# Sigmoid attention and a SwiGLU block on one core: transposes queued behind their casts, an earlier weight slice, and three copies shared by two engines

## The chip, the cores and the metric

The kernel runs on one core of a Trainium2 chip. The metric is the device time of one execution in microseconds (us); lower is better. The core has five engines that run side by side and meet only through semaphores: TensorE (PE in the profile, its weight loads PEld), VectorE (DVE), ScalarE (ACT), GpSimd (POOL) and SyncE (SP). SP computes nothing here; it issues transfers, in program order. POOL issues transfers too, also in program order with its own computing.

## The reference

```python
# q, k, v: (8, 12, 448, 64) float32
scores = scale * q @ k.T - log(448)          # scale = 1/8
attn   = 1 / (1 + exp(-scores))              # sigmoid attention, no row sums
x      = (attn @ v) -> (3584, 768)           # 8*448 tokens, 12 heads side by side
g      = x @ w_gate                          # 768 x 1536
out    = (g * sigmoid(g) * (x @ w_val)) @ w_out   # 1536 x 768, result (3584, 768) float32
```

## The kernel before, in words

**Attention is cut into quads.** A quad `n` is four heads of one batch entry: 8 batch entries times `NJ` = 3 quads give `NQ` = 24. For each quad, `fetch(n)` issues three loads on POOL's queue: q and k in float32 into the staging tile `stg_a` (four slots, two quads), and v, converted on the way, into `v` (five buffers). `casts(n)` are two POOL instructions (line 190) that turn q and k into bf16 tiles `c` (pool `c16`, four buffers, so two quads). `trans(n)` issues two DMA transposes on SP's queue (line 197) from `c` into `T` (pool `qkT`, three buffers for q and three for k). `ready(n)` is `casts(n)` followed by `trans(n)`. The first four quads are prepared in other ways during the ramp.

From `T` the PE makes score tiles `(n, c)`, seven per quad (line 239); ACT applies the sigmoid to each (`sig_tile`, lines 255 and 258) into `pt_a`; `pv(n)` multiplies with v on the PE (line 272), 28 matmuls, and copies the result to `xT` tiles: one 128x448 copy (line 281) and two of 64x448 (line 286). A parameter `how` of `pv` gives one of the two small copies to ACT (line 297, `how` = 1) in place of DVE; then `pv` returns a function `rest` that has to be called to make that copy.

**The block runs beside it.** `ffn1(b, f)` makes the gate and value products of batch entry `b` and hidden slice `f` (line 311), ACT the sigmoid (line 329), DVE the products (lines 331 and 335), giving `hT`. The second product of a pair of batch entries `pb` is made by one plain tile or several, `ffn2(pb, m)` (24 matmuls at line 606, then two DVE copies with a scale at line 619, one for each half of 384 columns, into an `osb` tile), and by `ffn2_group(pb, g)`, a Strassen-like form that makes two output tiles from seven half-size products (line 548, DVE at lines 559 and 565). There are six plain tiles: three for `pb` 0 and one for each other `pb`. The last `pb` uses a seven-product form for the first product as well (`double`, line 415). `osb` has four buffers; each is written out by two stores on SP's queue (line 518).

**PSUM** is a ring of four tiles of two banks (`ps_D`), handed out in program order by `Banked`. A unit waits until the earlier user of its tile has been read.

**The order is written out by hand.** Two lists are merged by estimated times: the units (`ffn1`, `ffn2`, ...) and the *visits*, groups of three or four score tiles: visit `(n, 0)` holds tiles 0 to 3 of quad `n`, visit `(n, 4)` tiles 4 to 6. After a visit that holds tile `(n, c)`, what stands in the dictionary `plan` under `(n, c)` is issued. For the later quads, `plan` puts `casts(n + 2)` and `fetch(n + 3)` at `(n, 4)`, and `trans(n + 2)` one visit later, at `(n + 1, 0)`. Stores of the units between those two visits are issued on SP's queue ahead of the transposes. For quads 6 to 9 `plan` calls `ready`, and `hold(n)`, a copy of one column out of `T` on POOL (line 734), makes POOL wait until the transposes of quad `n` have landed before the next `fetch`. `w_out(i)` loads slice `i` of four of the output weights (`wo`, line 130), also on POOL's queue. In `pb` 0's output stage `w_sum` (line 476) makes differences of those slices on DVE.

In the main loop a finished quad's `pv` is postponed to the next visit, or, ahead of certain units, issued alone; the flag `how` is true only for the second unit after the last visit, the last Strassen group of `pb` 2; in front of it the last quad's `pv(23)` is issued. Three operations of `x_sums` on POOL and the units `double` come after it.

Of the kernel before, what the change touches and what calls it, by code (L numbers as in the profile page):

```python
# [13 lines left out]
MULT = mybir.AluOpType.mult  # L14
# [6 lines left out]
def kernel(  # L21
# [10 lines left out]
    nc = tc.nc  # L32
    ctx.enter_context(tc.manual_schedule())

    B, H, S, D = q.shape
# [9 lines left out]
    hsc = lambda pb: 512.0 if pb in FAST else 4096.0  # L45
# [67 lines left out]
    def apart(second, *firsts):  # L113

        for first in firsts:
            keys[0] += 1
            tc.add_to_no_dep_group(f"half{keys[0]}", first.ins)
            tc.declare_no_dep(second.ins, group=f"half{keys[0]}", reason="another bank or other partitions")
# [102 lines left out]
    def trans_pe(n):  # L221
        D2 = Banked()
        ds = [qkT.tile([128, C, 128], BF16, tag=f"T{w}", name=f"T{w}_{n}") for w in range(2)]
        for f in [trans_part(D2, w, n, w, 0, C, nc.vector, ds[w]) for w in range(2)]:
            f()
        qT[(n, 0)] = ds[0]
# [34 lines left out]
    def pv(n, how=0, at=None):  # L261

        b, j = divmod(n, NJ)
        P = Banked(at=at).t
        vt = v16.pop(n)
        for c in range(C):
            pt = pts.pop((n, c))
            for h2 in range(2):
                for w in range(2):
                    r = slice(w * 64, w * 64 + 64)  # L270
                    g = (w ^ h2) * 64
                    nc.tensor.matmul(  # L272
                        out=P[g:g + 64, h2, :S],
                        lhsT=vt[r, h2, c * D:(c + 1) * D],
                        rhs=pt[r, h2, :],
                        start=(c == 0),
                        stop=(c == C - 1),
                    )

        x = xtp.tile([128, S], FP16, tag="xT", name=f"xT_{b}_{2 * j}")  # L280
        first = nc.vector.tensor_copy(out=x, in_=P[:, 0, :S])  # L281
        xT[(b, 2 * j)] = x
        x = xtp.tile([128, S], FP16, tag="xT", name=f"xT_{b}_{2 * j + 1}")
        xT[(b, 2 * j + 1)] = x
        halves = [(x[w * 64:(w + 1) * 64, :], P[(1 - w) * 64:(2 - w) * 64, 1, :S]) for w in range(2)]
        done = [nc.vector.tensor_copy(out=o, in_=i) for o, i in halves[how:]]  # L286
        if how == 2:
            for o, i in halves:
                apart(nc.scalar.copy(out=o, in_=i), first)
        sums = lambda: x_sums(b // 2, j) if b // 2 in FAST and b % 2 else None  # L290
        if how != 1:
            sums()

        def rest():
            if how == 1:
                o, i = halves[0]
                apart(nc.scalar.copy(out=o, in_=i), first, *done)
                sums()

        return rest  # L300


    V, G = nc.vector, nc.gpsimd
# [43 lines left out]
    hw = DM // 2  # L347
# [25 lines left out]
    def early_w(s):  # L373
        for kind in (3, 1, 2, 4):
            for i in range(JT):
                fast_w(s, kind, i)
# [3 lines left out]
    def x_sums(pb, j):  # L380

        a11, a12 = xT[(2 * pb, 2 * j)], xT[(2 * pb, 2 * j + 1)]
        a21, a22 = xT[(2 * pb + 1, 2 * j)], xT[(2 * pb + 1, 2 * j + 1)]
        if j == 0:
            ts = [half_of(ramp_a)[:, 8 * FW * hw + i * S:8 * FW * hw + (i + 1) * S] for i in range(3)]
        else:
            ts = [xtp.tile([128, S], FP16, tag="xT", name=f"xS{i}_{pb}_{j}") for i in range(3)]
        s1, s2, s4 = ts
        eng = G if j else V
        eng.tensor_tensor(out=s1, in0=a21, in1=a22, op=ADD)  # L390
        eng.tensor_tensor(out=s2, in0=s1, in1=a11, op=SUB)
        eng.tensor_tensor(out=a21, in0=a11, in1=a21, op=SUB)  # L392
        eng.tensor_tensor(out=s4, in0=a12, in1=s2, op=SUB)
        xS[(pb, j)] = (s1, s2, a21, s4)
# [114 lines left out]
    def store(engs, pb, m, osb, cols):  # L509

        for w in range(2):
            store_half(engs[w], pb, m, w, osb, cols)
# [85 lines left out]
    def ffn2(pb, m):  # L598
        D = Banked("o")

        head, tail = range(NF - 1), (NF - 1,)
        for half, fs in ((0, head), (1, head), (0, tail), (1, tail)):
            for f in fs:
                h = hT[(pb, f)].rearrange("p b s -> p (b s)")
                D.write(
                    nc.tensor.matmul(  # L606
                        out=D.t[:, half, :hw],
                        lhsT=h[:, m * 128:(m + 1) * 128],
                        rhs=wo16[f // FW][:, f % FW, half * hw:(half + 1) * hw],
                        start=(f == 0),  # L610
                        stop=(f == NF - 1),
                    ),
                    half,
                    uses=(pb, f),
                )
        osb = osp.tile([128, DM], FP32, tag="osb", name="osb")
        for half in range(2):
            D.read(
                nc.vector.tensor_scalar(
                    out=osb[:, half * hw:(half + 1) * hw], in0=D.t[:, half, :hw], scalar1=1.0 / hsc(pb), scalar2=None, op0=MULT  # L620
                ),
                half,
            )
        store((nc.sync, nc.sync), pb, m, osb, slice(0, DM))
# [37 lines left out]
    for grp in visits:  # L662
        n, c = grp[0]
# [7 lines left out]
    def attn_step(group, pvs, how):  # L671
        for part in (group[:2], group[2:]):
            scs = [(n, c, qk_tile(n, c)) for n, c in part]
            rest = [pv(pvs.pop(0), how) for _ in range(len(pvs))]
            for i, (n, c, sc) in enumerate(scs):

                sig_tile(n, c, sc, split=len(group) == 4 and part[0] == group[0] and i == 1)
            for f in rest:
                f()
# [121 lines left out]
    for f, Df in enumerate(early):  # L801
# [7 lines left out]
    plan = {  # L809
        (3, 2): ((casts, 5), (post.append, 4)),  # L810
        (3, 4): ((post.append, 5),),
        (4, 0): ((fetch, 6),),
        (4, 4): ((ready, 6),),
        (5, 4): ((hold, 6), (fetch, 7), (w_out, 0)),
        (6, 0): ((ready, 7),),
        (6, 4): ((hold, 7), (fetch, 8), (w_out, 1)),
        (7, 0): ((ready, 8),),
        (7, 4): ((hold, 8), (fetch, 9), (w_out, 2), (w_out, 3)),
        (8, 0): ((ready, 9), (fetch, 10)),
        (8, 4): ((casts, 10),),  # L820
        (9, 0): ((trans, 10), (fetch, 11)),
    }
    for n in range(9, NQ):
        if n + 2 < NQ:
            plan[(n, 4)] = ((casts, n + 2),)
            plan[(n + 1, 0)] = ((trans, n + 2),)
        if n + 3 < NQ:
            plan[(n, 4)] += ((fetch, n + 3),)

# [25 lines left out]
    for at, (fn, args, how) in enumerate(seq):  # L855
        if fn is None:
            pvs, pend = pend, []
            attn_step(args, pvs, how)
            if at == last_visit:
                nc.scalar.preload_act_table(SILU)  # L860
            for n, c in args:
                for act, of in plan.get((n, c), ()):
                    act(of)
                if c == C - 1:
                    pend.append(n)
            while post:
                trans_pe(post.pop())
            continue
        if pend and (fn is ffn1 and args[1] == 0 and (args[0], NP - 1) not in xT or fn is double or how):
            for n in pend:  # L870
                pv(n)
            pend = []
        fn(*args)
        if fn is ffn2 and args == (B // 2 - 2, C - 1):
            G.tensor_copy(out=held[:, :1], in_=hS[(args[0], 4, HF - 1)][:, :1])
            early_w(0)
        if fn is ffn2_group and args == (B // 2 - 2, 0):
            early_w(1)
# [30 lines left out]
```

## Time and profile before

| what | value |
|---|---|
| median of 9 runs | 410.42 us |
| lowest, highest | 408.88, 419.63 us |
| the profiled execution, its own time | 413.47 us |
| its span (first to last instruction) | 410.4 us, so 3.07 us lie around it |
| PE busy | 397.8 us (97%) |
| DVE, ACT, POOL busy | 263.2 (64%), 216.4 (53%), 126.1 us (31%) |
| mean granted PE clock | 0.995 |

The PE is the engine to follow: where it is busy, nothing else can shorten the kernel but less PE work, and where it is idle, the releaser of the next PE instruction names what was late. Idle time on the other engines costs nothing by itself. The profiled execution is itself 3.05 us slower than the median, so a wait seen in it need not have the same length in every run.

### The profile page before, as it was taken

Reading aid. Unit: us, or ns where it says so; the run is one execution under the profiler, and the core shown is the slowest. Engines: PE = TensorE matmul, PEld = TensorE weight load, DVE = VectorE, ACT = ScalarE, POOL = GpSimd, SP = SyncE. Lnnn points to the kernel's source line nnn. Section 1 sums busy time; section 2 is a strip of 40 time slices with the busy share of each in tenths; the row PEclk is TensorE's granted clock in tenths of the full one; section 3 lists DMA queues with packets and bytes.
Section 4 is the critical chain, followed back from the end, with each engine's and each line's share of the span. In section 5 each row is a group of like instructions: output and inputs, shape, how many; then the busy total and the mean of one; then the engine's idle time right before and its main releaser. Section 6 shows DMA issues by size and latency. Waiting matters only on the chain.

```text
span 410.4 us, 7992 instructions
## 1 busy us (share of the span) xinstructions
PE 397.8 (97%) x3158; PEld 206.6 (50%) x3158; DVE 263.2 (64%) x495; ACT 216.4 (53%) x332; POOL 126.1 (31%) x163
## 2 busy tenths in 40 slices
PE   7799999999999899999999999999999999999995
PEld 3345544545555444454555545445455555555563
DVE  2637646778855555677844565468775568996753
ACT  5866786646335474565543556555644325656100
POOL 4528042372621346330012314300019960000000
PEclk9899999999999999999999999999999999999999
DMA  8999969979899999742147799601001530000135
GB/s 260 250 250 249 238 129 136 202 171 228 229 188 160 235 226 169 211 69 91 22 85 205 158 229 158 157 17 30 1 2 46 140 86 0 2 1 0 40 82 148
DMA packets 59844, 54.38 MB, mean 132 GB/s; under 512 B 35744, under 2 KB 53280, under 8 KB 59808
## 3 DMA queue, kind: packets, MB, share of 16 engines
q0 software_dynamic: 18880, 30.94, 35.3%
q1 hardware_dynamic: 40496, 22.62, 27.6%
q8 instruction: 24, 0.39, 0.4%
q10 hardware_dynamic: 432, 0.33, 0.3%
q14 instruction: 12, 0.10, 0.1%
HBM read 47.19 MB, written 11.01 MB: 142 GB/s over the span
## 4 chain that ended last, share of the span: by engine, by line
PE 87%; DMA 8%; DVE 2%; SPq 1%; issue 0%; POOL 0%; DVEq 0%
PE ps_D L311 40%; PE ps_D L548 15%; PE ps_D L415 12%; PE ps_D L272 8%; PE ps_D L239 8%; DMA T<-c 5%; PE ps_D L606 5%; DMA v<-in_v_dram 2%; DMA st<-in_q_dram 1%; SPq L197 1%; DVE xT L286 1%; PE ps_D L209 0%; DVE xT L281 0%; DVE T L215 0%; SPq L518 0%
## 5 line engine op out<-in xcount | busy, mean ns | idle before, releaser
L258 ACT ACTIVATE pt_a<-ps_D 128x896 f16<-128x896 f32 x148 | 127.3, 919 | 77.4 <-PE ps_D L239 75.0
L311 PE MATMUL ps_D<-xT,wg 128*128 128x448 f16 x432 | 95.3, 353 | 0.1
L311 PE MATMUL ps_D<-xT,wv 128*128 128x448 f16 x432 | 94.8, 352 | 0.0
L331 DVE TENSOR_TENSOR t<-ps_D,s 128x448 f16<-128x448 f32 x72 | 44.8, 623 | 54.7 <-ACT s L329 53.5
L190 POOL CAST c<-stg_a 128x896 bf16<-128x896 f32 x40 | 38.3, 966 | 109.3 <-DMA T<-c 62.2
L329 ACT ACTIVATE s<-ps_D 128x448 f16<-128x448 f32 x72 | 39.5, 549 | 52.5 <-PE ps_D L311 45.9
L311 PEld LDWEIGHTS <-wg 128*128 128x128 f16 x432 | 39.6, 98 | 44.6 <-issue 11.3
L311 PEld LDWEIGHTS <-wv 128*128 128x128 f16 x432 | 42.2, 98 | 39.5 <-issue 0.4
L335 DVE SCALAR_TENSOR_TENSOR hT<-ps_D,t 128x448 f16<-128x448 f32 x72 | 45.0, 625 | 7.5
L239 PE MATMUL ps_D<-T,T 64*64 64x448 bf16 x644 | 44.5, 359 | 3.9 <-DMA T<-c 2.0
L272 PE MATMUL ps_D<-pt_a,v 64*64 64x448 f16 x672 | 36.9, 357 | 0.8 <-DMA v<-in_v_dram 0.8
L559 DVE TENSOR_SCALAR osb<-ps_D 128x384 f32<-128x384 f32 x43 | 24.0, 557 | 17.7 <-PE ps_D L548 17.0
L548 PEld LDWEIGHTS <-S 128*128 128x128 f16 x264 | 25.8, 98 | 17.8 <-issue 0.8
L548 PE MATMUL ps_D<-ramp_a,S 128*128 128x384 f16 x198 | 34.0, 326 | 0.6 <-DVE osb L559 0.6
L281 DVE CAST xT<-ps_D 128x448 f16<-128x448 f32 x24 | 15.0, 624 | 25.4 <-PE ps_D L272 25.2
L425 ACT ACTIVATE snap<-ps_D 128x448 f32<-128x448 f32 x36 | 18.6, 542 | 19.5 <-POOL xT L392 13.2
L239 PEld LDWEIGHTS <-T 64*64 64x64 bf16 x644 | 15.0, 106 | 26.4 <-issue 16.8
L565 DVE SCALAR_TENSOR_TENSOR osb<-ps_D,osb 128x384 f32<-128x384 f32 x33 | 18.4, 557 | 13.2 <-PE ps_D L548 13.1
L272 PEld LDWEIGHTS <-v 64*64 64x64 f16 x672 | 19.7, 108 | 14.0 <-DMA v<-in_v_dram 1.3
L548 PEld LDWEIGHTS <-hT 128*128 128x128 f16 x198 | 18.7, 98 | 14.6 <-issue 2.9
L286 DVE CAST xT<-ps_D 64x448 f16<-64x448 f32 x41 | 25.5, 621 | 0.7
L183 POOL DMA_DIRECT2D v<-in_v_dram x24 | 17.9, 746 | 25.5 <-PE ps_D L239 24.1
(84 smaller groups left out, 402.9 us busy)
## 6 DMA issues: line engine op xcount, KB each, us to landing
out_dram<-osb SPq DMA_DIRECT2D x52, 192.0 KB, 3.1
stg_a<-in_q_dram POOLq DMA_DIRECT2D x20, 448.0 KB, 4.8
stg_a<-in_k_dram POOLq DMA_DIRECT2D x20, 448.0 KB, 6.3
v<-in_v_dram POOLq DMA_DIRECT2D x24, 224.0 KB, 8.2
wg<-in_moe_w_gate_dram POOLq DMA_DIRECT2D x4, 576.0 KB, 11.9
wv<-in_moe_w_val_dram POOLq DMA_DIRECT2D x4, 576.0 KB, 13.0
wo<-in_moe_w_out_dram POOLq DMA_DIRECT2D x4, 576.0 KB, 8.6
ramp_a<-in_q_dram SPq DMA_DIRECT2D x2, 448.0 KB, 6.4
```

The source lines that it names most:

```text
L190: eng.tensor_copy(out=t.rearrange("p c h d -> p h c d"), in_=st.rearrange("p h (c d) -> p h c d", c=C))
L239: nc.tensor.matmul(out=sc[w * 64:(w + 1) * 64, h2, :S], lhsT=kt[r, w * 64:(w + 1) * 64], rhs=qt[r, :, w * 64:(w + 1) * 64], start=True, st ...
L258: nc.scalar.activation(out=pt, in_=sc[:, :, :S], func=SIGM, bias=sbias, scale=qkscale)
L272: nc.tensor.matmul(out=P[g:g + 64, h2, :S], lhsT=vt[r, h2, c * D:(c + 1) * D], rhs=pt[r, h2, :], start=(c == 0), stop=(c == C - 1),)
L286: done = [nc.vector.tensor_copy(out=o, in_=i) for o, i in halves[how:]]
L311: nc.tensor.matmul(out=D.t[:, i, :S], lhsT=(wg16, wv16)[i][f // FW][:, pr, cs], rhs=xT[(b, pr)], start=(pr == 0), stop=(pr == NP - 1),),
L329: D.read(nc.scalar.activation(out=s16, in_=D.t[:, 0, :S], func=SIGM), 0)
L331: D.read(nc.vector.tensor_tensor(out=t1, in0=D.t[:, 0, :S], in1=s16, op=MULT), 0)
L335: nc.vector.scalar_tensor_tensor(out=hT[(b // 2, f)][:, b % 2, :], in0=D.t[:, 1, :S], scalar=hsc(b // 2), in1=t1, op0=MULT, op1=MULT),
L415: nc.tensor.matmul(out=D.t[:, bank, :S], lhsT=W(f, j), rhs=X(j), start=(start and j == 0), stop=(stop and j == JT - 1), skip_group_check=True,
L548: nc.tensor.matmul(out=D.t[:, bank, :hw], lhsT=l, rhs=B_(i), start=(first and i == 0), stop=(i == HF - 1), skip_group_check=True,),
L559: nc.vector.tensor_scalar(out=o, in0=D.t[:, bank, :hw], scalar1=1.0 / hsc(pb), scalar2=None, op0=MULT), bank
```

## The change

Four edits. The transposes of quads 10 to 23 are issued in the same visit as their casts, at `(n, 4)` in place of `(n + 1, 0)`. The order of casts and loads on POOL does not change by it. The third slice of the output weights is loaded at `(6, 4)`, behind the second slice, in place of `(7, 4)`. In `ffn2` the first half of a plain output tile is copied and scaled by ACT in place of DVE. Where `pv` is issued alone for the last quad (flag `how`), it is called with `how` = 1 and its `rest` at once, so that one 64x448 copy goes to ACT.

```diff
@@ ffn2
         for half in range(2):
+            o, i, by = osb[:, half * hw:(half + 1) * hw], D.t[:, half, :hw], 1.0 / hsc(pb)
             D.read(
-                nc.vector.tensor_scalar(
-                    out=osb[:, half * hw:(half + 1) * hw], in0=D.t[:, half, :hw], scalar1=1.0 / hsc(pb), scalar2=None, op0=MULT
-                ),
+                V.tensor_scalar(out=o, in0=i, scalar1=by, scalar2=None, op0=MULT) if half else
+                nc.scalar.mul(out=o, in_=i, mul=by),
                 half,
             )
@@ plan
-        (6, 4): ((hold, 7), (fetch, 8), (w_out, 1)),
+        (6, 4): ((hold, 7), (fetch, 8), (w_out, 1), (w_out, 2)),
         (7, 0): ((ready, 8),),
-        (7, 4): ((hold, 8), (fetch, 9), (w_out, 2), (w_out, 3)),
+        (7, 4): ((hold, 8), (fetch, 9), (w_out, 3)),
         (8, 0): ((ready, 9), (fetch, 10)),
-        (8, 4): ((casts, 10),),
-        (9, 0): ((trans, 10), (fetch, 11)),
+        (8, 4): ((ready, 10), (fetch, 11)),
     }
     for n in range(9, NQ):
         if n + 2 < NQ:
-            plan[(n, 4)] = ((casts, n + 2),)
-            plan[(n + 1, 0)] = ((trans, n + 2),)
+            plan[(n, 4)] = ((ready, n + 2),)
         if n + 3 < NQ:
             plan[(n, 4)] += ((fetch, n + 3),)
@@ main loop
             for n in pend:
-                pv(n)
+                pv(n, 1 if how else 0)()
             pend = []
```

## The prediction

> **What bounds the kernel now.** I first read the page for the engine and the chain.
>
> ```profile
> PE 397.8 (97%) x3158; PEld 206.6 (50%) x3158; DVE 263.2 (64%) x495; ACT 216.4 (53%) x332; POOL 126.1 (31%) x163
> PE 87%; DMA 8%; DVE 2%; SPq 1%; issue 0%; POOL 0%; DVEq 0%
> L239 PE MATMUL ps_D<-T,T 64*64 64x448 bf16 x644 | 44.5, 359 | 3.9 <-DMA T<-c 2.0 <-DVE T L215 1.2 <-ACT pt_a L258 0.3
> L548 PE MATMUL ps_D<-ramp_a,S 128*128 128x384 f16 x198 | 34.0, 326 | 0.6 <-DVE osb L559 0.6
> ```
>
> The PE is idle for 410.4 - 397.8 = 12.6 us. A table of busy time by stretches of 10 us tells where: 5.5 us before 30, 4.4 after the last matmul, and between 30 and 400 only three stretches are under 10.00: 9.86 (120 to 130), 8.01 (130 to 140) and 9.40 (320 to 330). So the middle holds 0.14 + 1.99 + 0.60 = 2.73 us, and nothing else in the middle can be won without less PE work. The change removes no matmul, and it touches neither end. The timeline names the two large gaps, in brackets:
>
> ```profile
> 137.79 0.57 PE L239 MATMUL ps_D<-T,T 64*64 64x448 bf16 x8 [1.99 <-DMA T<-c]
> ```
> ```profile
> 326.23 0.62 DVE L281 CAST xT<-ps_D 128x448 f16<-128x448 f32 x1 [0.97 <-PE ps_D L272]
> 326.87 1.25 DVE L286 CAST xT<-ps_D 64x448 f16<-64x448 f32 x2
> 328.15 0.56 DVE L559 TENSOR_SCALAR osb<-ps_D 128x384 f32<-128x384 f32 x1
> 328.77 3.08 PE L548 MATMUL ps_D<-ramp_a,S 128*128 128x384 f16 x18 [0.60 <-DVE osb L559]
> ```
>
> The first is visit (11, 0), which waits for a transpose of quad 11. Why that is late stands in SP's timeline and, for the start of each piece, in the chain in order of time:
>
> ```profile
> 104.29 5.57 SPq L518 DMA_DIRECT2D out_dram<-osb  x4
> 109.97 4.84 SPq L197 DMA_TRANSPOSE T<-c  x2
> 114.90 8.24 SPq L518 DMA_DIRECT2D out_dram<-osb  x6
> 123.25 5.45 SPq L197 DMA_TRANSPOSE T<-c  x2
> 130.10 2.44 SPq L518 DMA_DIRECT2D out_dram<-osb  x4
> ```
> ```profile
> 123.25 1.59 SPq L197
> ...
> 124.93 12.82 DMA T<-c
> ```
>
> Quad 11's casts ran on POOL from 105.66 to 108.58, but its transposes stood on SP behind stores that wait for DVE's `osb`, and went out at 123.25 and 124.93. The second landed 12.82 us later, at 137.75; the PE was ready at 135.80. Quad 10 is the same case by a hair: cast by 101.6, issued from 109.97, landed at 121.20, wanted at 121.1 (the 0.14 us). The second gap is DVE's own order after `pv(23)`: three `xT` copies (0.62 us each) stand ahead of the copy at line 559 that must free a PSUM bank.
>
> **What the Trainium skill says.** "Perfetto Trace Analysis", section Optimization Strategy: find the gaps on the contended engine, find which semaphore each waits for, and make that dependency start sooner. That is the reading above. "DMA: Bandwidth & Descriptors", section Queues, rings and completion order: a DMA engine takes its queues in turn, packet by packet. The trace agrees: while loads were queued (93 to 98 us), quad 9's transposes moved about 110 packets per us beside about 112 of the loads; alone (68 to 69) they moved 748. So an early transpose may still land late behind loads, and I price that. "ScalarE: Activation LUTs", section Table sets: plain copies are in every table set, so the copies given to ACT need no further table load. The trace agrees: ACT's snap copies at line 425 run between SILUs, with two loads in all (1.283 us each).
>
> **Part by part.**
>
> *Transposes at (n, 4).* The order of instructions on SP changes from stores x4, T10, x6, T11, x4, T12 to T10, x6, T11, x8, T12 (Tn: the two transposes of quad n). T10 can go at about 101.6, when its casts end; SP is idle then (quad 9's last issue ended at 96.8). T11 stands behind six stores, the last of which waits for the third plain tile (copied by 114.45), so it goes near 115 in place of 123.25: 8 us sooner. With the slowest landing in the trace (13.9 us, quad 9's) the second lands by 115 + 1.6 + 13.9 = 130.5, before 135.8. Both waits go: **-2.13 us** (1.99 + 0.14). T12 keeps its place behind the eight stores, so it is next in line: issued at 132.64 and 136.3, landed 9.2 and 8.8 us later, at 145.1; wanted at 150.05, and with the gap gone at 148.06. Slack 2.9 us. From quad 13 on, the PE waited for none; all go out no later than before. SP also waits for PE now (T of quad n+2 needs quad n-1's buffer): that reader is a visit older than any store queued behind, so no store is held by it. What can hold a store is a late cast: T17's was done by 169.6, T18's by 183.7, long before the stores at 208 and 216. Faster casts afterwards (POOL waited 62.2 us for `T<-c`) only bring loads forward; POOL is on no path there.
>
> *Third weight slice at (6, 4).* One POOL issue (0.80 us) moves ahead of quad 8's casts, where POOL idles 1.48 us for q (75.36): nothing on POOL. Its transfer moves from behind fetch 9 to behind slice two. Slice two took from about 77 to 80.7 at some 175 KB/us, so 576 KB are 3.3 us more load traffic, until 84. T8, which lands at 83.4 before, then gets half the packets for 3.3 us and lands near 86.5. `hold(8)` holds POOL for the same 3 us, so fetch 9, its casts and T9 (issued 88.8 and 90.3) start 3 us later; but the loads ahead of T9 are the slice fewer. T9 landed at 104.2, wanted at 107.2: I take 0, with bounds 0 to +2.3 (a start 5.3 later and again 13.9 to land: 109.5). The slices: two lands sooner; slice four moves up by one transfer and back by the 3 us, so it stays near 97.9; its first matmul is at 100.8.
>
> *Plain tiles.* Six DVE copies (0.55 us) become six on ACT (nearest row: line 425, 542 ns). The PE waited for none of them, so 0 is won directly; the tile is out some 0.5 us sooner. New wait: ACT stands at the tile's end with the next visit's sigmoids behind it, and the PE behind those for a PSUM tile. At `pb` 1:
>
> ```profile
> 207.12 1.02 DVE L619 TENSOR_SCALAR osb<-ps_D 128x384 f32<-128x384 f32 x2 [2.03 <-PE ps_D L606]
> 207.61 0.92 ACT L258 ACTIVATE pt_a<-ps_D 128x896 f16<-128x896 f32 x1 [2.16 <-PE ps_D L239]
> ```
>
> ACT's copy would run 207.1 to 207.66, so the sigmoid starts 0.05 late and ends at 208.6; the PE wants that tile at about 209.15, after `pv`. Covered by 0.5 us at all four places followed by a visit: 0. Without that cover it would be 4 x 0.55 = 2.2.
>
> *PV copy.* DVE does two of the three `xT` copies, so line 559 runs from 327.5 to 328.07; the PE, which ended six more matmuls at 328.17, no longer waits: **-0.60 us** (bounds 0 and -0.60). ACT is idle there (1.23 us of work between 320 and 330). `x_sums` starts on POOL at 331.27 after its own queue either way; the sum that product 6 needs ends at 333.42, wanted at about 335.3 in place of 335.9: covered.
>
> Sum: -2.73 us; 413.47 becomes 410.7 in the profiled execution, 3.05 above the median. The PV wait is fixed durations and counts fully in the median. The transpose wait is a race: the landing had 10.9 us from issue, and the six landings of quads 9 to 11 took 13.2, 13.9, 10.6, 9.7, about 12.5 and 12.8, mean 12.1, so a typical wait is 1.2 to 2.1. I take 1.6: 410.42 - 1.6 - 0.6 = **408.2 us**.
>
> **Rivals.**
>
> *A. The forecast*: both waits go. 407.2 to 409.2. Chance 0.52.
>
> *B. The transpose wait is not there in the median run, or T11 is not really sooner* (POOL or a buffer holds it). For it: the profiled run is 3.05 us slow, and something must be shorter in the others. Against: 4 of 6 landings exceed 10.9. Only 0.6 stays: 409.8. Chance 0.22.
>
> *C. T9 is late at (9, 0)*, behind the moved slice. Decides from a delay of 3.0 us; up to +2.3: 408.2 + 2.3 = 410.5, less where it is partly so. Chance 0.10.
>
> *D. Slower: T12 is late at (12, 0)*, because loads run ahead now and share the DMA engines with it. Decides when T12 lands over 2.9 us later than before. With quad 9's worst issue (6.52 us) and landing (13.9): 132.64 + 6.52 + 13.9 = 153.1, a wait of 5.0: 408.2 + 5.0 = 413.2. For it: quad 9 shows such values. Against: casts 14 wait for T12 itself, so only one fetch can be ahead. Chance 0.11. Unlisted harm: 0.05, near 412.
>
> **How the numbers follow.** 0.3% (1.23 us) is about what a measurement of this kernel can tell from no change: below 409.2 is faster, above 411.6 slower. Faster: A and a third of C, 0.55. Same: B and half of C, 0.27. Slower: D, the rest of C and the unlisted, 0.18. Range: 406.9 (A with a wait of 2.9 us, which is the landing of 13.9 against 10.9, in the median) to 411.9, which leaves out most of D.
>
> **What would show it.** In the profile after: no stretch under 10.00 between 120 and 140; T10 issued near 102 and T11 near 115; no wait of PE at 328, with a line-297 copy on ACT beside DVE's; six scaled copies on ACT of about 0.54 us, and the sigmoid behind each at most 0.1 late. Wrong: a PE wait for `T<-c` at visit (9, 0) or (12, 0), for `pt_a` after a plain tile, or a span that shrinks by 2.7 us while the median doesn't move (then B).

## The result and the profile after

The changed kernel takes 415.05 us in the median (17 runs, 411.06 to 418.67), the kernel before 410.28 us (52 runs, 408.62 to 419.84): 4.8 us or 1.2% slower. The ratio is 1.0099, 95% interval 1.0076 to 1.0121. (Ratios leave out runs more than 1.5% above the fastest of the same kernel, and as a late transfer alone can push a run over that line here, the medians of all runs are given beside them.) The forecast was 408.2 us: a gain of 2.2 us where a loss of 4.8 came.

The page of the kernel after, engines and chain:

```profile
PE 398.5 (97%) x3158; PEld 206.8 (50%) x3158; DVE 259.9 (63%) x488; ACT 219.8 (53%) x339; POOL 125.7 (31%) x163
PE 72%; DMA 21%; POOL 4%; issue 1%; SPq 0%; DVE 0%; POOLq 0%; DVEq 0%
L239 PE MATMUL ps_D<-T,T 64*64 64x448 bf16 x644 | 44.4, 359 | 5.9 <-DMA T<-c 4.2
L548 PE MATMUL ps_D<-ramp_a,S 128*128 128x384 f16 x198 | 34.0, 326 | 0.0
```

The share of transfers in the chain rose from 8% to 21%. The idle time in front of line 548 is 0.0 (it was 0.6), so that part worked; in front of line 239 it grew from 3.9 to 5.9 us. The timeline of the PE shows a single wait between 30 and 404 us:

```profile
97.91 7.97 PE L606 MATMUL ps_D<-wo,hT 128*128 128x384 f16 x48
110.12 0.64 PE L239 MATMUL ps_D<-T,T 64*64 64x448 bf16 x8 [4.24 <-DMA T<-c]
110.53 2.84 PE L272 MATMUL ps_D<-pt_a,v 64*64 64x448 f16 x28
...
114.01 4.07 PE L606 MATMUL ps_D<-wo,hT 128*128 128x384 f16 x24
```

This is visit (9, 0): the PE is ready at 110.12 - 4.24 = 105.88 and waits until a transpose of quad 9 has landed. The gap at (11, 0) is gone. The same place in the kernel before:

```profile
107.20 0.57 PE L239 MATMUL ps_D<-T,T 64*64 64x448 bf16 x8
107.60 1.49 PE L272 MATMUL ps_D<-pt_a,v 64*64 64x448 f16 x28
...
109.41 4.08 PE L606 MATMUL ps_D<-wo,hT 128*128 128x384 f16 x24
```

There is a second loss behind the wait. The 28 matmuls of `pv` take 2.84 us, 1.49 in the kernel before. Busy time by stretch (its length, then PE, PEld, DVE, ACT and POOL, then the granted clock, the DMA share and GB/s; the DMA share can pass 1, as it adds up the times of packets that overlap) names the reason:

```profile
110.50:113.90 3.40, 3.40 (x41) 1.55 (x32) 0.45 (x1) 2.28 (x4) 1.64 (x3) 0.50 0.74 172
```

Half the clock for 3.4 us. From the start of (9, 0) to the next plain tile the PE took 2.21 us before (107.20 to 109.41) and takes 3.89 now (110.12 to 114.01): 1.68 us more. The whole loss at this place is 4.24 + 1.68 = 5.9 us.

The chain in order of time, from 76 us, tells how quad 9 came to be late:

```profile
78.03 9.19 DMA T<-c
...
87.34 0.19 POOL held L734
...
88.57 5.74 DMA stg_a<-in_k_dram
...
94.36 0.94 POOL c L190
...
95.32 14.75 DMA T<-c
```

For the kernel before, line 197 shows the transposes of quad 8 and of quad 9 (how many, min/median/max ns to issue them, start of the first and the last; then the us from issue to landing):

```profile
L197 SPq DMA_TRANSPOSE T<-c x2: 1431/1514/1597, 76.3 to 77.9; - x2
DMA to landing us min/median/max: 5.5/5.8/6.2
...
L197 SPq DMA_TRANSPOSE T<-c x2: 1369/3943/6517, 88.8 to 90.3; - x2
DMA to landing us min/median/max: 13.2/13.6/13.9
```

Quad 8's second transpose now takes 9.19 us to land (5.5 before), with the third weight slice beside it. `hold(8)` on POOL waits for it until 87.3, so fetch 9 starts at 87.82 (83.95 before). The second transpose of quad 9 goes out at 95.32 (90.3 before), and then takes 14.75 us. It took 13.9 before: the start is what moved.

The span grew by only 1.7 us (410.4 to 412.1): the removed waits give 2.7, the new one takes 5.9, and the profiled execution after had a faster ramp, which reached (9, 0) 1.3 us sooner. Between medians the difference is 4.8, which the experiments split into 6.1 lost and 1.3 won.

### The profile page after: what moved, and what is told of

It is laid out like the page before. It is cut to its first block, busy times and chain, and to the rows that moved or that the text cites. A ratio compares the mean times of both kernels' runs of the same rounds, so it can differ in the third digit from the quotient of the medians.

```text
span 412.1 us, 8001 instructions
## 1 busy us (share of the span) xinstructions
PE 398.5 (97%) x3158; PEld 206.8 (50%) x3158; DVE 259.9 (63%) x488; ACT 219.8 (53%) x339; POOL 125.7 (31%) x163
## 4 chain that ended last, share of the span: by engine, by line
PE 72%; DMA 21%; POOL 4%; issue 1%; SPq 0%; DVE 0%; POOLq 0%; DVEq 0%
PE ps_D L311 27%; PE ps_D L548 18%; PE ps_D L415 12%; DMA stg_a<-in_k_dram 11%; DMA T<-c 8%; PE ps_D L239 6%; PE ps_D L272 5%; PE ps_D L606 4%; POOL c L190 2%; DMA ramp_a<-in_q_dram 1%; POOL stg_a L178 1%; POOL wg L133 1%; POOL wv L133 1%; POOL v L183 0%; SPq L161 0%
## 5 line engine op out<-in xcount | busy, mean ns | idle before, releaser
L311 PE MATMUL ps_D<-xT,wg 128*128 128x448 f16 x432 | 95.3, 353 | 0.1
L559 DVE TENSOR_SCALAR osb<-ps_D 128x384 f32<-128x384 f32 x43 | 24.0, 558 | 17.5 <-PE ps_D L548 16.8
L272 PEld LDWEIGHTS <-v 64*64 64x64 f16 x672 | 19.8, 109 | 13.9 <-issue 1.6
## 6 DMA issues: line engine op xcount, KB each, us to landing
wg<-in_moe_w_gate_dram POOLq DMA_DIRECT2D x4, 576.0 KB, 11.9
```

What stands on the lines that cost most here:

```text
L272: nc.tensor.matmul(out=P[g:g + 64, h2, :S], lhsT=vt[r, h2, c * D:(c + 1) * D], rhs=pt[r, h2, :], start=(c == 0), stop=(c == C - 1),)
L311: nc.tensor.matmul(out=D.t[:, i, :S], lhsT=(wg16, wv16)[i][f // FW][:, pr, cs], rhs=xT[(b, pr)], start=(pr == 0), stop=(pr == NP - 1),),
L559: nc.vector.tensor_scalar(out=o, in0=D.t[:, bank, :hw], scalar1=1.0 / hsc(pb), scalar2=None, op0=MULT), bank
```

## The experiments

Each run was measured beside new runs of the kernel before, whose medians lie between 410.1 and 410.8 us; a ratio compares with these.

The first question was which of the edits costs the time. Theory: the moved slice. Rival: the transposes issued sooner.

**The changed kernel without the slice move** (`no_slice`).

```diff
-        (6, 4): ((hold, 7), (fetch, 8), (w_out, 1), (w_out, 2)),
+        (6, 4): ((hold, 7), (fetch, 8), (w_out, 1)),
-        (7, 4): ((hold, 8), (fetch, 9), (w_out, 3)),
+        (7, 4): ((hold, 8), (fetch, 9), (w_out, 2), (w_out, 3)),
```

> The changed kernel with the third weight slice put back to (7, 4). Slice theory (the moved slice delays T8, hold(8), fetch 9 and so the transposes of quad 9, and the PE then idles 4.2 us at visit (9, 0) and runs 1.7 us more at half clock): those 6 us go; the profile has no PE wait for T at (9, 0), none at (11, 0) and none at 328; time 0.6 to 2.7 us under the kernel before, ratio 0.993 to 0.998. Transpose theory (transposes 10 and 11 issued earlier share the DMA engines with the loads and make those of quad 9 late): still 3 us or more slower than before, ratio over 1.007, with the wait at (9, 0).

Measured: 408.94 us (22 runs, 407.94 to 413.51), ratio 0.9966 (0.9940 to 0.9992). Between 30 and 404 us its PE has no wait at all; its page:

```profile
PE   7799999999999999999999999999999999999995
PE 94%; DMA 2%; DVE 1%; ACT 1%; SPq 0%; issue 0%; DVEq 0%; ACTq 0%
```

The other three edits make the kernel faster by 1.3 us in the median; the slice move takes 6.1 (415.05 - 408.94). With the earlier transposes kept, the wait is gone: the rival falls.

**The slice move alone** (`slice_only`): the same two lines changed the other way, in the kernel before.

> The kernel before with the third weight slice alone moved to (6, 4). Slice theory: T8 lands 3 to 4 us later, the second transpose of quad 9 is issued near 95 in place of 90.3 and lands near 110; PE wait of 3 to 4.5 us at (9, 0) and half clock behind it; the wait at (11, 0) may stay; 4 to 6 us slower, ratio 1.010 to 1.015. Transpose theory: within 1 us of the kernel before, ratio 0.998 to 1.002.

Measured: median 415.95 us (22 runs, 409.22 to 425.72), 5.7 over the kernel before. The ratio, in which only its seven fastest runs count, is 1.0052 (1.0012 to 1.0093). Its timeline:

```profile
112.59 0.96 PE L239 MATMUL ps_D<-T,T 64*64 64x448 bf16 x8 [5.65 <-DMA T<-c]
143.64 0.57 PE L239 MATMUL ps_D<-T,T 64*64 64x448 bf16 x8 [1.34 <-DMA T<-c]
```

The wait at (9, 0) is there without the moved transposes, and the two old waits are there too: 1.34 at (11, 0), and 0.60 for line 559 at 334.6. The second transpose of quad 9 was issued at 94.26 and took 18.28 us.

**The moved transposes alone** (`trans_only`), the hunks at (8, 4) and in the loop over `n`.

```diff
-        (8, 4): ((casts, 10),),
-        (9, 0): ((trans, 10), (fetch, 11)),
+        (8, 4): ((ready, 10), (fetch, 11)),
...
-            plan[(n, 4)] = ((casts, n + 2),)
-            plan[(n + 1, 0)] = ((trans, n + 2),)
+            plan[(n, 4)] = ((ready, n + 2),)
```

> The kernel before with the transposes of quads 10 to 23 alone moved behind their casts. Slice theory: transposes 10 near 102 and 11 near 115, the waits of 0.14 and 1.99 us are gone, ratio 0.994 to 1.000. Transpose theory: slower by 3 us or more, ratio over 1.007, with a PE wait for T near 107 or at a later visit.

Measured: median 409.48 us, ratio 0.9980 (0.9954 to 1.0006), not told from 1 by itself. There is no PE wait for `T<-c` in its trace, but this trace alone says little on that: it is of one of its longer executions (413.55 us), in which the PE was late already, by a wait before (9, 0):

```profile
102.72 8.18 PE L606 MATMUL ps_D<-wo,hT 128*128 128x384 f16 x39 [2.72 <-DMA wo<-in_moe_w_out_dram]
```

There a weight slice came late at the first plain tile. So an earlier slice answers to something that does happen, in some executions.

**The copies alone** (`copies_only`), the hunks in `ffn2` and in front of `pv`.

```diff
-                nc.vector.tensor_scalar(
-                    out=osb[:, half * hw:(half + 1) * hw], in0=D.t[:, half, :hw], scalar1=1.0 / hsc(pb), scalar2=None, op0=MULT
-                ),
+                V.tensor_scalar(out=o, in0=i, scalar1=by, scalar2=None, op0=MULT) if half else
+                nc.scalar.mul(out=o, in_=i, mul=by),
...
-                pv(n)
+                pv(n, 1 if how else 0)()
```

> The kernel before with the plain-tile copies and the PV copy alone split over ACT and DVE. Both theories: the 0.60 us PE wait near 328 goes, nothing else moves; 0.6 us faster, ratio 0.9985, which may not be told from 1.

Measured: median 409.16 us, ratio 0.9986 (0.9966 to 1.0005): the 0.6 us expected by the ratio (1.1 by the medians), and within the noise. The wait at 328 is gone. Its trace has a wait that the kernel before's trace didn't have, at (12, 0):

```profile
148.22 0.57 PE L239 MATMUL ps_D<-T,T 64*64 64x448 bf16 x8 [1.33 <-DMA T<-c]
```

The transposes alone and the copies alone add to 0.8 + 0.6 = 1.4 us by their ratios; both together (`no_slice`) gave a ratio of 0.9966, 1.4 us. That fits parts that add up, but with intervals of about 1 us to each side it doesn't show it.

**Each copy by itself** (`pv_only`, `plain_only`), one profiled execution each.

> The kernel before with the PV copy alone shared: the PE wait of 0.60 us near 328 goes.

> The kernel before with the plain-tile copies alone shared: the PE wait of 0.60 us near 328 stays; no new PE wait for a sigmoid (pt_a) behind the plain tiles.

Measured: with the PV copy shared, there is no wait near 328, and one of 0.39 us at 113.6, in front of line 548, for a plain tile's copy at line 619. With the plain tiles shared, the 0.60 stays, and no wait for `pt_a` appears:

```profile
124.58 0.96 PE L239 MATMUL ps_D<-T,T 64*64 64x448 bf16 x8 [4.00 <-DMA T<-c]
332.62 3.08 PE L548 MATMUL ps_D<-ramp_a,S 128*128 128x384 f16 x18 [0.60 <-DVE osb L559]
```

So the 0.60 is the PV copy's. This execution took 416.04 us: with the order of transposes as before, quad 10's second one went out at 110.4, took 14.1 us, and the PE waited 4.00 at (10, 0). The kernel before has the same order, so some of its runs of 414 to 417 us may come about in this way; none of these was profiled.

The second question was how one slice of 576 KB, moved by one quad, makes quad 9 late. Two links were in doubt: `hold(8)`, and fetch 10 beside the transposes.

**Fetch 10 held until quad 9's transposes have landed** (`after_hold9`), in the changed kernel.

```diff
-        (8, 0): ((ready, 9), (fetch, 10)),
+        (8, 0): ((ready, 9), (hold, 9), (fetch, 10)),
```

> The changed kernel with hold(9) put between the transposes of quad 9 and fetch 10, so that POOL issues fetch 10 only when those transposes have landed. If the transposes of quad 9 are late because fetch 10 shares the DMA engines with them: issued near 92.5 and 95.3 as in the changed kernel, they land near 102 in place of 110, and the PE wait of 4.2 us at (9, 0) and the half clock behind it go; fetch 10 starts near 102.5 and quad 10 is still in time; about 409 us, ratio 0.996 to 1.000. If their late issue alone decides (some 14 us to land whatever is beside them): they land near 109 again, and it stays 4 us or more slower than before.

Measured: 410.16 us (14 runs), ratio 1.0002 (0.9979 to 1.0026), 4.9 us under the changed kernel. The transposes of quad 9 went out at 92.1 and 93.9, later by 3.3 and 3.6 us than in the kernel before (92.6 and 95.3 in the changed kernel), and landed in 6.5 and 5.5 us. The view of line 197 for quads 8 and 9:

```profile
L197 SPq DMA_TRANSPOSE T<-c x2: 1291/2436/3582, 75.8 to 77.2; - x2
DMA to landing us min/median/max: 8.4/8.8/9.2
...
L197 SPq DMA_TRANSPOSE T<-c x2: 1523/1600/1677, 92.1 to 93.9; - x2
DMA to landing us min/median/max: 5.5/6.0/6.5
```

Quad 8's (first pair) are still slow behind the slice; quad 9's are not. With nothing of fetch 10 beside them they land at 99.4, seven us before the PE wants them (106.38). From 93.9, a landing of 14.75 us would have been 2.3 us too late. So fetch 10 beside the transposes is part of the cause.

**Without `hold(8)`** (`after_nohold8`), in the changed kernel.

```diff
-        (7, 4): ((hold, 8), (fetch, 9), (w_out, 3)),
+        (7, 4): ((fetch, 9), (w_out, 3)),
```

> The changed kernel without hold(8): fetch 9 is issued right behind quad 8's casts, near 78 in place of 87.8. If the way from the moved slice to quad 9 leads through hold(8): casts 9 near 90, transposes of quad 9 issued near 91 and landed by 105, no PE wait at (9, 0) beyond 1 us; 409 to 411 us. Quad 8's own transposes share the engines with slice and fetch 9 and may land near 90 where the PE wants them at 90.5 to 91.8. If hold(8) is not the link: the wait of 4 us at (9, 0) stays, 414 us or more.

Measured: 415.28 us (6 runs), ratio 1.0114 (1.0076 to 1.0152). The wait moved by one quad:

```profile
96.06 0.96 PE L239 MATMUL ps_D<-T,T 64*64 64x448 bf16 x8 [4.81 <-DMA T<-c]
```

This is (8, 0). Now fetch 9 runs beside quad 8's transposes, and they take 13.6 and 16.8 us. Quad 9's went out at 89.4 and 91.5, the second 3.8 us sooner than in the changed kernel, and landed by 105.5. That fits the link through `hold(8)`. That the PE no longer waited for them says little, as it came to (9, 0) only at 114.27. What the run shows besides is that the hold does a service: without it the same collision happens one quad sooner.

**Both slices at (6, 4)** (`after_two_slices`), in the changed kernel: twice the suspected cause.

```diff
-        (6, 4): ((hold, 7), (fetch, 8), (w_out, 1), (w_out, 2)),
+        (6, 4): ((hold, 7), (fetch, 8), (w_out, 1), (w_out, 2), (w_out, 3)),
-        (7, 4): ((hold, 8), (fetch, 9), (w_out, 3)),
+        (7, 4): ((hold, 8), (fetch, 9)),
```

> The changed kernel with the fourth weight slice moved to (6, 4) too, behind the third: twice the suspected cause. Through hold(8): T8 lands another 3 us later (near 90), fetch 9 is issued near 91, T9 near 97 and 99, landing at 111 to 113; PE wait at (9, 0) of 5 to 7 us; 1 to 4 us slower than the changed kernel, ratio to before 1.013 to 1.022. If the bytes in front of T9 decide and not the hold (the fourth slice no longer stands between fetch 9 and T9): no slower than the changed kernel.

Measured: 409.09 us (20 runs, 408.02 to 410.97), ratio 0.9957 (0.9937 to 0.9976). No PE wait between 30 and 404 us. I had expected 1 to 4 us more than the changed kernel; it is 6 less. The delay of the start came as expected: `hold(8)` held until 90.4, and quad 9's transposes went out at 95.9 and 97.2, later than in the changed kernel:

```profile
L197 SPq DMA_TRANSPOSE T<-c x2: 1221/1233/1245, 95.9 to 97.2; - x2
DMA to landing us min/median/max: 3.3/5.6/7.9
```

But they landed in 3.3 and 7.9 us, the last at 105.1, and the PE wanted it at 106.48. Fetch 10 was issued beside them here too (97.11). So the delay by itself is not what costs: late transposes with a short landing are in time. The fourth slice, left between fetch 9 and quad 9's transposes, belongs to the cause as well.

**Both slices in the kernel before** (`two_slices_only`).

```diff
-        (6, 4): ((hold, 7), (fetch, 8), (w_out, 1)),
+        (6, 4): ((hold, 7), (fetch, 8), (w_out, 1), (w_out, 2), (w_out, 3)),
-        (7, 4): ((hold, 8), (fetch, 9), (w_out, 2), (w_out, 3)),
+        (7, 4): ((hold, 8), (fetch, 9)),
```

> The kernel before with both the third and the fourth slice moved to (6, 4). If the slice that stays between fetch 9 and quad 9's transposes is what makes the single move costly: no wait at (9, 0); the waits at (11, 0) and at 328 stay; within 0.3% of the kernel before, ratio 0.997 to 1.001, beside about 1.014 in the medians for the third slice alone. If two slices are only in time because the transposes of the later quads moved: a wait at (9, 0), ratio over 1.007.

Measured: 410.02 us, ratio 0.9998 (0.9979 to 1.0018). No wait at (9, 0). One slice alone costs 5.7 us in the medians, two cost nothing, whatever the order of the later transposes. Its profiled execution took 416.97 us, with 3.58 us of waiting at (11, 0): the old wait, longer than in the first trace.

**The fourth slice between quad 9's casts and fetch 10** (`after_fourth_later`, and the same kernel again as `fourth_later_2` and `fourth_later_3`).

```diff
-        (7, 4): ((hold, 8), (fetch, 9), (w_out, 3)),
+        (7, 4): ((hold, 8), (fetch, 9)),
-        (8, 0): ((ready, 9), (fetch, 10)),
+        (8, 0): ((ready, 9), (w_out, 3), (fetch, 10)),
```

> The changed kernel with the fourth slice moved from in front of quad 9's casts to between these casts and fetch 10: the same transfers in front of fetch 10, but quad 9's q and k no longer share with the slice, and its transposes then run beside the slice and ahead of most of fetch 10. If the q and k loads beside the transposes make them slow: the second transpose of quad 9 lands within 10 us (by about 104), no wait for T at (9, 0); a wait of 0 to 3 us for the fourth slice at the first plain tile is possible, as that now lands near 100 or later; 408.5 to 412 us. If the bytes queued decide, whatever they are: T9 lands near 109 again, 414 us or more.

Measured: median 413.05 us in two groups (6 runs up to 410.2, 16 from 411.2), ratio 1.0042 (1.0016 to 1.0068). The trace was of an execution of 409.12 us, so two more were profiled:

> The same kernel as after_fourth_later, a second look. If its time is over 411 us: either a PE wait for the fourth slice (wo) near 100, 2 us or more with half clock behind it, and T9 landed in time; or a wait for T at (9, 0), near 107, of 2 us or more, with T9 landed near 109.

> A third look at the same kernel, with the same alternatives.

They took 415.15 and 411.10 us. Each has one wait of the PE, and it is for the slice:

```profile
103.90 8.97 PE L606 MATMUL ps_D<-wo,hT 128*128 128x384 f16 x39 [3.79 <-DMA wo<-in_moe_w_out_dram]
```
```profile
102.44 6.50 PE L606 MATMUL ps_D<-wo,hT 128*128 128x384 f16 x39 [2.76 <-DMA wo<-in_moe_w_out_dram]
```

The second transpose of quad 9 took 12.1, 11.9 and 12.4 us in the three traces and landed between 105.8 and 108.1. That is neither "within 10" nor "109 again": beside a slice and then fetch 10 it is faster than in the changed kernel and slower than with less company. No sharp difference between q, k loads and weights was shown.

**Hold(9) without the slice move** (`no_slice_hold9`), the line of `after_hold9` added to `no_slice`.

> The changed kernel with the slice put back to (7, 4) and hold(9) ahead of fetch 10: a version that may beat both. Transposes of quad 9 land near 99 in place of 104, quad 10's still before 119; no PE wait between 30 and 400 us: median 408 to 409.5, as without hold(9) or a little under, with fewer runs over 411. If fetch 10 comes too late for quad 10: a wait at (10, 0), 410 or more.

Measured: 409.68 us, ratio 0.9986 (0.9963 to 1.0010), 0.7 us over `no_slice` in the median and with 4 of 22 runs over 411.5. The profiled execution (412.57 us) waited 0.62 us for a weight slice and 1.55 us for `osb` at 120.7. Where quad 9 is in time already, holding fetch 10 gained nothing. The second transpose of quad 9 landed in 9.7 us here (13.4 in `no_slice`).

**The best of these**: `no_slice` (408.94 us, ratio 0.9966) and `after_two_slices` (409.09 us, 0.9957) both beat both kernels. They were measured beside different runs of the kernel before (medians 410.27 and 410.76), and their intervals overlap, so they are not told apart. The second has no run over 410.97.

## Why the prediction was wrong, point by point

**The waits that were to go did go.** At (11, 0) and at 328 the PE waits no longer. The PV term, -0.60, is exact in the trace and fits the copies' ratio of 0.9986. The transpose term, taken at -1.6 for a typical run, measures -0.8 (`trans_only`, interval -1.9 to +0.2): twice too large by the middle value, as rival B had it in part, but within the interval. Together they measure 1.4 where 2.2 was forecast.

**The step that failed is the third weight slice**: "I take 0, with bounds 0 to +2.3". It measures about +6 (6.1 from `no_slice`, 5.7 from `slice_only`, in medians; 5.9 in the trace). Its mechanism, rival C (quad 9 late at (9, 0) behind the moved slice), was the right one and was given 0.10 and at most +2.3. Three of its terms were wrong.

- *The cancelling.* I let T9's later start be paid back by "the loads ahead of T9 are the slice fewer". The start moved by more than the 3 us that I took: 3.8 for the first transpose and 5.0 for the second (the bound had 5.3). And the landing of the second didn't shorten; it went from 13.9 to 14.75. The table has that landing in every trace that bears on it, by the weight slices issued between fetch 9 and T9, and by where fetch 10 was issued.

| slices ahead of T9 | fetch 10 issued beside T9 | fetch 10 held until T9 has landed |
|---|---|---|
| two | 13.0 to 14.4 us (six traces, the kernel before and `no_slice` among them) | 9.7 us (`no_slice_hold9`) |
| one | 14.75 us (changed kernel), 18.28 us (`slice_only`), 14.0 us (`after_nohold8`) | 5.5 us (`after_hold9`) |
| none | 7.9 us (`after_two_slices`), 7.8 us (`two_slices_only`) | not tried |

With fetch 10 held, a slice fewer does shorten the landing, as I had it. With fetch 10 beside T9, one slice fewer doesn't, and two slices fewer do. That fetch 10 is issued in the same us as T9 (95.24 and 95.32) was in the order of POOL's instructions, and it was so in the kernel before (89.94 and 90.3), but I priced it only for rival D. The two columns differ by one held load, but each cell of the second rests on one trace.

The other two terms:

- *The moment wanted.* Landing was bounded at 109.5 and measured at 110.07, near enough. But I set it against 107.2, the PE's arrival in one execution; in this one the PE came at 105.88. The slack of 3.0 us (104.2 to 107.2) loses 1.3 by the ramp alone.
- *The clock.* I counted a wait as its own length. A wait of 4.24 us brought 1.68 us more at half clock.

**Rival D** (T12 late at (12, 0)) didn't happen in the changed kernel; a wait of 1.33 there turned up in `copies_only`. **The plain tiles** cost nothing, as forecast: ACT's copies take 0.49 us (forecast 0.54), and at `pb` 1 the sigmoid starts right behind the copy with no wait for `pt_a` on the PE:

```profile
209.46 0.49 ACT L621 ACTIVATE osb<-ps_D 128x384 f32<-128x384 f32 x1 [1.67 <-PE ps_D L606]
209.95 0.92 ACT L258 ACTIVATE pt_a<-ps_D 128x896 f16<-128x896 f32 x1
```

But "the tile is out some 0.5 us sooner" didn't come true. DVE's copy of the second half waits for ACT's copy of the first, here at the third plain tile:

```profile
117.96 0.49 ACT L621 ACTIVATE osb<-ps_D 128x384 f32<-128x384 f32 x1 [2.27 <-PE ps_D L606]
118.48 0.56 DVE L620 TENSOR_SCALAR osb<-ps_D 128x384 f32<-128x384 f32 x1 [1.36 <-ACT osb L621]
```

The profile gives ACT's copy as the releaser at five of the six tiles. The two engines take turns, so a pair lasts some 1.1 us, as with two copies on DVE (1.02 at 207.12). In front of line 559 the two engines do overlap (ACT's 64x448 copy at 328.48, DVE's copies at 328.59 and 329.23), and there the wait went.

**The issue times** were off: T10 went at 105.2 and 110.0 in place of 102, T11 at 120.3 in place of 115. Fetch 10 was issued 5.3 us later than before, and POOL then waited until 109.07 for its k; T11 stands behind stores of the third plain tile, which the PE reached late. In `no_slice` T10 went at 101.5 and 102.8 and T11 at 114.5, as forecast.

**What stays open.** That the slice move costs the 6 us is shown, and that both the slice left ahead of T9 and fetch 10 beside it take part. Why the landing stays at 13 us and more with fetch 10 beside and one slice or two ahead, is some 12 with the fourth slice behind the casts, and 8 with none ahead, is not settled. It isn't a matter of bytes alone: over 98 to 110 us the changed kernel's transfers moved 143 GB/s at a DMA share of 1.14, and before, in the like stretch from 92 to 104, 211 GB/s at 1.04. In `slice_only` they moved 49 GB/s from 98 to 100 and 74 from 100 to 102, at shares of 1.38 and 1.41. Why the mixture is so slow was not tried.

## What to carry to other kernels

Before moving a load, list everything that waits for the queue it joins, including a pacing wait that was put there by design, and follow the delay to the next collision; compare not the bytes but which transfers will now be in flight together. A transfer that gets fewer bytes ahead of it need not land sooner: a later start was not paid back here. A slack read from one execution has to be lessened by the spread of the ramp and of the landing times, both over 1 us here. And price a long PE wait with the slow clock behind it: here it came with each of the six waits of 3.58 us and more.

## What the runs showed of the hardware that I had not expected

- *Landing times of the same transpose spread more than fivefold.* A transpose of a 128x896 tile of quad 9 landed in 3.3 us in `after_two_slices`, with no weight slice ahead of it, and in 18.28 us in `slice_only`, with one ahead and fetch 10 beside it.
- *A long PE wait costs more than itself.* With waits of 3.58 us and more the granted clock was 0.50, for 3.4 us (4.24 and 5.65 us of wait) or about 6.8 (3.58, 3.79, 4.00 and 4.81). With 2.72 us it fell in one trace and with 2.76 it stayed at 1.00 in another; after 30 us, no wait of 1.99 or less in these traces brought it down. The slow stretch can begin inside the wait: in `plain_only` it began near 123.2, and the wait ended at 124.58. An example for each length, of `slice_only` and of `plain_only`:

```profile
112.00:115.30 3.30, 2.71 (x32) 1.37 (x36) 0.00 (x0) 1.79 (x3) 2.88 (x4) 0.50 1.38 137
```
```profile
123.20:126.50 3.30, 1.92 (x24) 0.96 (x28) 0.00 (x0) 1.21 (x2) 2.22 (x3) 0.50 1.08 359
126.50:129.90 3.40, 3.40 (x32) 1.42 (x25) 1.24 (x2) 2.25 (x5) 1.76 (x3) 0.50 1.14 287
```
